# Two moves at the seam between attention and mixture of experts: one VectorE instruction later, one gather earlier

## The chip, the cores and the metric

The kernel runs on one core of one Trainium2 chip. The metric is the device time of one execution in microseconds (us). The engines are named as in the profile: PE (TensorE matmuls), PEld (its weight loads), DVE (VectorE), ACT (ScalarE), POOL (GpSimd) and SP (SyncE, which here only issues transfers).

## The reference

Causal attention with a cumulative bias over 8 batches of 8 heads (576 positions, 64 dimensions per head), whose output is the input of a mixture of 8 experts. Each of the 4608 rows goes to the one expert with the highest cosine similarity.

```
scores = q @ k^T / sqrt(D);  cum = cumsum(max(s, 0))
scores = where(causal, -1e9, scores + min(-(cum_i - cum_j), 0))
attn   = softmax(scores);    x = (attn @ v) as rows [4608, 512]
logits = xn @ en^T / tau;    expert_idx = argmax(logits);  gate_w = softmax(logits)[expert_idx]
for e in range(8):
    h = relu(x[expert_idx == e] @ w1[e]);  out[expert_idx == e] = gate_w * (h @ w2[e])
```

## The kernel before, in words

**Attention.** The 64 heads are a software pipeline: `step(n)` issues the scores of head n, the exponentials, the split of the probabilities into a 16-bit main part and a 16-bit remainder, and the product with V of head n-2. The remainder of the probabilities, `pl_`, is computed in pieces, by POOL (`psub`, L252) or by DVE (L508). The product, `pv`, accumulates in one PSUM bank, `om`; DVE's `norm1` to `norm3` (L539, L543, L551) read it out into the row buffer `xt`, and the next head's `pv` waits for that.

**Routing.** After the last head of a batch, `router` sums the logits out of `xt` (L79), picks the expert (L608 to L623), ranks the rows with matmuls (`rank0`, L630 to L636), and POOL scatters the rows to a list per expert in DRAM (`scat`, L670).

**Experts.** An expert's rows come back in five blocks of 128 (blocks 0 to 4). `xload(e, t)` (L739) is an indirect gather that POOL issues, into one of three places of 580 words in the tile `Qx`: place t % 3. `xprep(e, t)` then transposes the block on PE (L767, four matmuls), splits it on ACT and DVE (L775, L783) and takes its statistics (L751 on ACT; L748, L749, L79 on DVE); after that the place is free. `l1` multiplies with w1 (L915, L917), `l2m` with w2 (L986), and `l2o` scales a finished block on DVE (L993) and has POOL scatter it to the output (L994). Expert 0 begins while the attention ends: `first_pass(m)` is block m of its hidden layer for the first 256 rows, and the other rows follow in two more passes.

**Weights.** SP loads 128x512 pieces of w1 and w2, numbered q in the order of use, into a ring of raw buffers (`rw` is the tile of pieces 0 to 2). ACT converts a piece to 16 bits (`wcv`, L881) and DVE takes the remainder (`wlow`, L889), which also lets SP load a later piece into the freed buffer. `wlow(k)` takes the oldest k remainders that are pending.

**Order.** Each engine executes its instructions in the order in which the Python code issues them: the order is written out by hand and no scheduler changes it. Around the change that code is `step(n)` for n = 62 and 63 (the last two heads; `wlow(1)` at L1244), the lines behind the loop (L1400 to L1412), the closures `third`, `fourth` and `fifth`, which are called from the middle of expert 0's second-layer blocks, and the loop over m in expert 0's last first-layer pass (L1535 to L1537). POOL's queue holds remainders of probabilities, scatters, gathers and output scatters in one line.

Of the kernel before, what the change touches and what calls it, by code (L numbers as in the profile page):

```python
# [41 lines left out]
XR = 580  # L42
# [72 lines left out]
def main(ctx, tc, qkh, qkc, vtin, s_in, emb, tau, w1h, w2h, out, shared, nb):  # L115
# [36 lines left out]
    NH, LA = nb * H, 5  # L152
# [580 lines left out]
            X[("i", e, t)] = (xf[:, i], (IX["gi0"][:, t:t + 1], IX["va0"][:, t:t + 1]) if e + t0 == 0 and t1 < NTL else (IX["gi"][:, e, t:t + 1], IX["va"][:, e, t:t + 1]), L[:, i], ss[:, i], ex[:, :, t - t0])  # L733

    def xload(e, t):
        x = HT["Qx"][:, XR * (t % 3):XR * (t % 3) + XR]
        early = e == 0 and t < NF
        src = xs[0:SPL if t < 2 else SPM, :] if early else xs
        ins = nc.gpsimd.indirect_dma_start(out=x.bitcast(I32), out_offset=None, in_=src, in_offset=bass.IndirectOffsetOnAxis(ap=X[("i", e, t)][1][0].bitcast(U32), axis=0),  # L739
                                           bounds_check=src.shape[0] - 1, oob_is_err=False).ins  # L740
        X[("r", e, t)] = x
        if early:
            firsts.append(ins)
# [41 lines left out]
    def xprep(e, t, pt=None):  # L785
        xset(e, t)
        x = X[("r", e, t)][:, 0:XW]
        if e > 1:
            if "xr" not in HT:
                HT["xr"] = const.tile([128, 2, 2, 4, 128], F16, tag="KC1", name="xr")  # L790
            rows = x.rearrange("p (q c) -> p q c", q=4)[:, :, 8:136]
            h, l = (HT["xr"][:, t % 2, i] for i in range(2))
            nc.scalar.copy(h, rows)
            nc.vector.tensor_tensor(l, rows, h, op=ALU.subtract)
            for o, r in ((X[("H", e)], h), (X[("L", e)][1], l)):
                nc.sync.dma_start_transpose(o[:, :, 128 * t:128 * t + 128], r.rearrange("p q c -> p (q c)"))
            return xstat(e, t)
        xtr(e, t, pt)
        xcv(e, t)
        xstat(e, t)  # L800
# [85 lines left out]
    def wlow(k=99):  # L886
        for _ in range(min(k, len(lows))):
            q, l, a, s, h = lows.popleft()
            nc.vector.scalar_tensor_tensor(l, a, s, h, op0=ALU.mult, op1=ALU.subtract)  # L889
            wissue(min(q + 15, X.get("hold", 16 * NE)))  # L890
# [308 lines left out]
    def step(n):  # L1199
        m = n + LA - (n < 6)  # L1200
        live = n < NH
        b0, b1, c8 = n // H, n // H + 1, n % H
        prev = n - 1 < NH
        g, c = n // HG, n % HG
        if live and c == 0:
            hset(g + 1)
            if n > 4:
                load(g + 2)
                loadc(g + 2)
        if n == 10:  # L1210
            setup4()
            setup3()
        fslot()
        norm1(n - 3)
        if live:
            ta_(n, m)
        if prev:
            pl_(n - 1, 576, PS(n), "p")
        sr(m, 3)
        norm2(n - 3)  # L1220
        sa(m)
        if live:
            expa(n)
            prep(n, True)
        norm3(n - 3)
        if NH - 7 < n < NH:
            brk[0] = False
            slots(4)
        if live:
            tb_(n)  # L1230
        sr(m, 2)
        if live and n % 2 == 0:
            tbm(n)
        s3(m)
        if live:
            if n % 2:
                tbm(n)
            tbl(n)
        if n < NH - 6 or n >= NH:
            mslot()  # L1240
        if prev and PS(n) < 1600:
            pl_(n - 1, PS(n), 1600, "v")
        if n < NH - 1:
            wlow(1)  # L1244
        k = n - NH + 8
        if k == 3:
            wsq(8, True)
        if n < NH - 1:
            emm(n)
        sb(n, m)  # L1250
        sbr(m)
        if n < NH:
            tail(n)
        if n == 5:
            s1(10)
            sr(10, 3)
            s2(10)
        if n == 7:
            vscale(1)
        pv(n - 2, [0, 1, 2])  # L1260
        if n == 7:
            fslot()
        if rq:
            rq.popleft()()
        if n == 5:
            sr(10, 2)
            sr(10, 1)
            s3(10)
        pv(n - 2, [3, 4])
        if n == NH - 1:  # L1270
            emm(n)
        if n == 5:
            s4(10)
        if NH - 7 < n < NH:
            mslot()
        if n >= NH - 1:
            for f in (norm1, norm2, norm3):
                f(n - 2)
        if live:
            expb1(n)  # L1280
            if k == 7:
                wsq(13)
            vcp(n, False)
        if k == 3:
            wsum(0)
        aslot()
        if n == 4:
            load(3)
            loadc(3)
        if live:  # L1290
            prep(n, False)
            vcp(n, True)
        if n == NH - 1:
            xcv(0, 0)
            xtr(0, 1, pxs())
            xcv(0, 1)
        if k > 0:
            wsq((0, 2, 5, 8, 9, 10, 11, 14)[k])
            wcv((0, 0, 0, 0, 2, 1, 2, 1, 1, 1, 0)[k], True)
        brk[0] = False  # L1300
        if n < NH - 6:
            slots(4)
        if n in (4, 5, 6):
            vsq(1, ((0,), (1, 2), (3,))[n - 4])
        if H <= n < NH and 2 <= c8 < 6 and b1 < nb:
            vsq(b1, (c8 - 2,))
        if live and c8 == 6 and 1 < b1 < nb:
            vscale(b1)
        if n == 3:
            loadt(1, pair(1))  # L1310
        if H <= n < NH and c8 < 4:
            loadt(b1, c8)
        if n == NH - 9:
            wissue(3)
        for _ in range(SCN[c8] if n < NH - 22 else 2 if NH - 3 < n < NH else 1 + (c8 > 5) + 4 * (n > NH - 6)):
            scatter()
        later()
        if live and c == 0:
            addl(g + 1, True)
        if live and c == 1:  # L1320
            addl(g + 1, False)
        mrow1(m)
        if live:
            pl_(n, 0, 576, "p")
# [81 lines left out]
    wlow(1)  # L1406
    first_pass(0)
    wsq(16)
    wlow(1)
    pv(NH - 1, range(5))  # L1410
    wn = wparts()
    wn.pop(0)()  # L1412
# [77 lines left out]
    def fifth():  # L1490
        size(0)
        xprep(1, 2, pxm())
        wsq(22)
    l2(0, 1, {2: third, 4: partial(l2o, 0, 0, y), 6: fifth})
    l2(0, 2, {2: fourth, 7: l1t})
# [2 lines left out]
    for e in range(NE):  # L1498
        nx = e + 1 < NE
        w2, w1 = 16 * e + 8, 16 * e + 16  # L1500
        for m in range(8):
            l1(m, e, 0 if e else SPM, MAIN)
            if e > 1 and m == 1:
                l2u(e - 1)
            if e == 1 and m == 0:
                l2o(0, NTL - 1, X["y", 0])
            if e and m == 2:
                size(e)
            if e == 1:
                wsq(w2 + (6, 7, 8)[m] if m < 3 else w1 + (0, 0, 0, 1, 4)[m - 3])  # L1510
                if m == 3:
                    wn = wparts()
                    for i, f in enumerate(X[("g", 1, 0)][4]):
                        if i < len(wn):
                            wn[i]()
                        f()
                wcv((1, 2, 1, 2, 2, 2, 2, 0)[m])
            elif e > 1:
                if e == 2 and m == 0:
                    wsq(w2 + 8)  # L1520
                    wnorm()
                if e == 2 and m < 5:
                    wcv(2 if m else 0)
                if e > 2 and m < 4:
                    wcv(2)
                if nx and m > 3:
                    wsq(w1 + 2 * (m - 3))
            if nx and e > 0 and m == 1:
                xinfo(e + 1, 0, NTL)
            if nx and e > 0 and m == 2:  # L1530
                for t in range(3):
                    xload(e + 1, t)
            if e == 0 and m in (2, 4, 6):
                wsq(24 + m // 2)
            if e == 0 and m in (1, 5):  # L1535
                xprep(1, m // 4, pxm())
                xload(1, 3 + m // 4)  # L1537
            if e > 1 and m < 4:
                X[("g", e, 0)][m]()
            if e == 1 and m in (0, 4, 7):  # L1540
                X[("g", e, 0)][{0: 0, 4: 2, 7: 3}[m]]()
            if not nx and m == 5:
                nc.gpsimd.drain()
            if not nx and m == 4:
                xf = X[("i", e, NTL - 1)]
                nc.vector.tensor_copy(shared["last"][:, 0:1].bitcast(I32), xf[0])
                nc.vector.tensor_mul(shared["last"][:, 1:2], xf[3], IX["RS"][:, 2 * e + 1:2 * e + 2])
            if nx and e > 0 and m in (5, 7):
                xprep(e + 1, m // 2 - 2)
                xload(e + 1, m // 2 + 1)  # L1550
            if e == 2 and m == 5:
                count()
            if e == 3 and m == 4:
                shared["total"] = nc.values_load(shared["ci"][0:1, NE - 1:NE], min_val=0, max_val=NT // 128)
# [170 lines left out]
```

## Time and profile before

| | us |
|---|---|
| median of 3 runs | 760.83 |
| lowest, highest | 760.51, 762.04 |
| the profiled execution | 760.35 |
| its span, first to last instruction | 758.6 |
| PE busy | 738.8 (97% of the span) |
| ACT busy | 567.7 (75%) |
| DVE busy | 531.3 (70%) |
| POOL busy | 396.7 (52%) |

The profiled execution lasts 1.75 us longer than its span. Attention ends near 347 us on PE, and the experts follow. Where the profile shows an idle time in square brackets, it is the idle time of that engine just before the instruction, and behind the arrow stands what ended it.

### The profile page before, as it was taken

To read this page: it belongs to the slowest core of one execution; us is meant where nothing else is said; L and a number is where in the kernel's file an instruction comes from. 1 tells how busy PE (TensorE), PEld (TensorE's weight loads), DVE (VectorE), ACT (ScalarE), POOL (GpSimd) and SP (SyncE) were. 2 spreads that over 40 slices of the span, in tenths; PEclk is the share of its full clock that TensorE was granted. 3 is DMA by queue.
4 is the path that set the end of the run, shared out by engine and by line. 5 is a ranking of instruction groups with operands and counts; after the bars stand their busy time and mean duration, and the time that the engine had idled before them with its cause. 6 is when DMAs were issued, how large, how long until landed. Compare 5 with 4: busy or idle time off the path is not lost. (4 is left out here: it accounts for less than half of the span.)

```text
span 758.6 us, 20953 instructions
## 1 busy us (share of the span) xinstructions
PE 738.8 (97%) x7992; PEld 536.2 (71%) x7992; DVE 531.3 (70%) x1818; ACT 567.7 (75%) x1029; POOL 396.7 (52%) x377
## 2 busy tenths in 40 slices
PE   8999999999999999989989999999999999999996
PEld 4799999999999999978555454545454554554554
DVE  8778888888888888898767767565665566745621
ACT  9898989898999999977667878737658578475410
POOL 9997898989897988685323212222221122312011
PEclk9999999999999999999999999999999999999999
DMA  7789879797979797763625956845755657553001
GB/s 151 176 191 193 172 181 204 179 208 170 210 182 207 165 221 164 183 225 138 213 91 182 191 162 195 185 131 151 178 173 132 189 173 194 168 128 96 13 15 58
DMA packets 76002, 124.01 MB, mean 163 GB/s; under 512 B 38823, under 2 KB 39231, under 8 KB 75032
## 3 DMA queue, kind: packets, MB, share of 16 engines
q0 software_dynamic: 19632, 69.69, 39.1%
q1 hardware_dynamic: 56260, 52.84, 25.8%
q8 instruction: 71, 1.16, 0.7%
q14 instruction: 39, 0.32, 0.2%
HBM read 93.99 MB, written 21.49 MB: 152 GB/s over the span
## 5 line engine op out<-in xcount | busy, mean ns | idle before, releaser
L252 POOL TENSOR_TENSOR PL<-P 128x576 f16<-128x576 f32 (+2 forms) x128 | 204.5, 1719 | 13.6 <-ACT P L498 9.1
L915 PE MATMUL pe<-xH,wt 128*128 128x512 f16 (+1 forms) x576 | 153.0, 344 | 0.6 <-PEq L1020 0.5
L994 POOL DMA_INDIRECT out<-Kx,xj x39 | 43.0, 1103 | 201.6 <-DVE Kx L993 164.3
L915 PEld LDWEIGHTS <-wt 128*128 128x128 f16 x960 | 86.0, 98 | 81.6 <-issue 2.0
L526 PE MATMUL om<-vh,P 128*128 128x73 f16 x960 | 106.8, 198 | 2.7 <-DVE xt L551 2.0
L527 PE MATMUL om<-vl,P 128*128 128x72 f16 x960 | 106.2, 196 | 0.0
L528 PE MATMUL om<-vh,PL 128*128 128x73 f16 x960 | 106.0, 197 | 0.0
L739 POOL DMA_INDIRECT Qx<-xs,idx x40 | 47.5, 1188 | 101.8 <-ACT vjunk L844 44.9
L362 PE MATMUL s<-qkb 96*128 96x288 f32 (+4 forms) x272 | 96.2, 368 | 1.9 <-DVE M L370 0.8
L527 PEld LDWEIGHTS <-P 128*128 128x128 bf16 x960 | 94.6, 99 | 3.6 <-issue 3.2
L915 PE MATMUL pe<-xL,wt 128*128 128x512 f16 (+1 forms) x288 | 95.6, 344 | 0.0
L526 PEld LDWEIGHTS <-P 128*128 128x128 bf16 x960 | 93.8, 99 | 0.5 <-DVE xt L551 0.3
L528 PEld LDWEIGHTS <-PL 128*128 128x128 f16 x960 | 93.8, 98 | 0.0
L917 PE MATMUL pxs<-xH,wt 128*128 128x64 f16 x432 | 83.2, 193 | 0.0
L370 DVE CUSTOM_DVE_ANT_0 junk<-s,mS 128x448 bf16<-128x448 f32 (+3 forms) x144 | 73.9, 520 | 5.0 <-PE s L362 2.8
L986 PE MATMUL pxs<-wt,hq 128*128 128x512 f16 x297 | 72.7, 379 | 0.0
L501 ACT ACTIVATE P<-tb 128x1024 f32<-128x1024 f32 x64 | 65.1, 1017 | 3.3 <-PE tb L467 1.9
L986 PEld LDWEIGHTS <-hq 128*128 128x128 f16 x360 | 35.3, 98 | 42.0 <-ACT idx L88 0.3
L917 PEld LDWEIGHTS <-wt 128*128 128x128 f16 x648 | 63.5, 98 | 0.4
L464 PE MATMUL tb<-QC,KC 128*128 128x448 f32 (+3 forms) x256 | 63.3, 306 | 0.0
L460 PE MATMUL tb<-qkb 128*128 128x448 f32 (+3 forms) x256 | 61.2, 287 | 0.0
L889 DVE SCALAR_TENSOR_TENSOR wt<-ring,idx,wt 128x512 f16<-128x512 f32 x80 | 56.8, 745 | 4.8 <-ACT wt L881 4.8
(335 smaller groups left out, 1997.0 us busy)
## 6 DMA issues: line engine op xcount, KB each, us to landing
qkb<-qkh POOLq DMA_DIRECT2D x15, 1216.0 KB, 9.1
ring<-w2h SPq DMA_DIRECT2D x44, 256.0 KB
ring<-w1h SPq DMA_DIRECT2D x36, 256.0 KB
KC<-qkh POOLq DMA_DIRECT2D x14, 576.0 KB, 8.9
QC<-qkh POOLq DMA_DIRECT2D x14, 576.0 KB, 8.5
vT<-vtin SPq DMA_DIRECT2D x24, 320.0 KB
rw<-w1h SPq DMA_DIRECT2D x15, 256.0 KB
rw<-w2h SPq DMA_DIRECT2D x12, 256.0 KB
```

The source lines that it names most:

```text
L252: nc.gpsimd.tensor_tensor(out, a, b_, op=ALU.subtract)
L362: nc.tensor.matmul(out, G[g]["QB"][0:96, h, 128 * i:128 * i + 128], G[g]["KB"][0:96, h, lo:hi], start=True, stop=True)
L370: nc.vector.tensor_tensor_reduce(out=jk, in0=src, in1=ms, scale=1.0, scalar=NEG, op0=ALU.add, op1=ALU.max, accum_out=MP[n // 2][:, n % 2, ...
L460: nc.tensor.matmul(out, G[g]["KB"][:, h, ks:ks + 128], G[g]["QB"][:, h, 64 + qlo:64 + qhi], start=start, stop=False)
L464: nc.tensor.matmul(out, HD[n]["KC"][:, ks:ks + 128], HD[n]["QC"][:, qlo:qhi], start=False, stop=stop)
L501: nc.scalar.activation(HD[n]["P32"][:, 576:1600], HD[n]["tb"], AF.Exp, scale=0.125)
L526: nc.tensor.matmul(out, lh, vh[:, kb], start=(kb == 0), stop=False)
L527: nc.tensor.matmul(out[:, u:u + 72], lh, vl[:, kb], start=False, stop=False)
L528: nc.tensor.matmul(out, ll, vh[:, kb], start=False, stop=(kb == j))
L915: nc.tensor.matmul(h, w[:, 128 * c:128 * c + 128], x[:, c, lo:hi], start=(i == 0), stop=(i == 11))
L917: nc.tensor.matmul(X["a"][:, HALF * m:HALF * m + HALF], w[:, 128 * c:128 * c + 128], x[:, c, hi:hi + HALF], start=(i == 0), stop=(i == 11))
L986: nc.tensor.matmul(y, h, w, start=(m == 0 and k == 0), stop=(m == 7 and k == 2))
```

## The change

Three things are edited. In `step(n)`, the remainder of one weight piece is no longer taken at n = 62 (the last step but one). Behind the loop, the second `wlow` call takes two remainders where it took one, so that the count is made up behind `first_pass(0)`. For expert 1 the gather of block 3 uses place 2 and that of block 4 place 0 (before: places 0 and 1). Block 3 is gathered from `fifth`, behind the preparation of expert 1's block 2; block 4 is gathered at m = 1 of expert 0's loop, where block 3 was gathered before, and nothing is gathered at m = 5. Instructions are neither added nor taken away.

```diff
     def xload(e, t):
-        x = HT["Qx"][:, XR * (t % 3):XR * (t % 3) + XR]
+        i = t % 3 if e != 1 or t < 3 else (t - 1) % 3
+        x = HT["Qx"][:, XR * i:XR * i + XR]
...
-        if n < NH - 1:
+        if n < NH - 2:
             wlow(1)
...
     wlow(1)
     first_pass(0)
     wsq(16)
-    wlow(1)
+    wlow(2)
     pv(NH - 1, range(5))
...
     def fifth():
         size(0)
         xprep(1, 2, pxm())
+        xload(1, 3)
         wsq(22)
...
             if e == 0 and m in (1, 5):
                 xprep(1, m // 4, pxm())
-                xload(1, 3 + m // 4)
+                if m == 1:
+                    xload(1, 4)
```

On DVE, in the steps 62 and 63 of the kernel before, the remainder of piece 1 (the tile `rw_176`) stands between a part of head 61's probability remainder (L508) and the V remainder of head 62 (L311), and `norm1` to `norm3` of head 60 follow:

```order
L551 TENSOR_TENSOR xt<-om,z 128x5x72
L508 TENSOR_TENSOR PL_111<-P_87 128x576
L889 SCALAR_TENSOR_TENSOR wt<-rw_176,idx,wt 128x512
L311 SCALAR_TENSOR_TENSOR vl<-V,sc,vh_109 128x3x144
L539 TENSOR_SCALAR z<-om 128x5
L543 RECIPROCAL z<-z 128x5
L551 TENSOR_TENSOR xt<-om,z 128x5x72
```

Behind the loop, DVE has in the kernel before the read-out of head 62, piece 2's remainder, the first hidden block's low part (L922), piece 3's remainder, and the read-out of head 63:

```order
L543 RECIPROCAL z<-z 128x5
L551 TENSOR_TENSOR xt<-om,z 128x5x72
L889 SCALAR_TENSOR_TENSOR wt<-rw_177,idx,wt 128x512
L922 SCALAR_TENSOR_TENSOR hp<-h,hp 128x256
L889 SCALAR_TENSOR_TENSOR wt<-wt,idx 128x512
L539 TENSOR_SCALAR z<-om 128x5
```

The same place of the changed kernel (its lines behind the edit in `xload` are one higher, so L889 is L890 there):

```order
L543 RECIPROCAL z<-z 128x5
L551 TENSOR_TENSOR xt<-om,z 128x5x72
L890 SCALAR_TENSOR_TENSOR wt<-rw_176,idx,wt 128x512
L923 SCALAR_TENSOR_TENSOR hp<-h,hp 128x256
L890 SCALAR_TENSOR_TENSOR wt<-rw_177,idx,wt 128x512
L890 SCALAR_TENSOR_TENSOR wt<-wt,idx 128x512
L539 TENSOR_SCALAR z<-om 128x5
```

Piece 1's remainder has gone from the first place to the second, where it stands ahead of the first hidden block, and piece 2's remainder has moved behind that block; the instructions in between have kept their order.

On POOL, in the kernel before, the queue from the gathers ahead of expert 0's second layer to those of expert 2 (L739 gathers, L994 scatters output):

```order
L739 DMA Qx<-xs,idx 128x580 x3
L1461 MEMSET ring 1x1
L739 DMA Qx<-xs,idx 128x580
L994 DMA out<-Kx,xj 4608x512 x2
L739 DMA Qx<-xs,idx 128x580
L957 UNCONDITIONAL_BRANCH
L994 DMA out<-Kx,xj 4608x512
L739 DMA Qx<-xs,idx 128x580 x2
L967 UNCONDITIONAL_BRANCH
```

The same stretch of POOL's queue in the changed kernel (L740 and L995 are the gathers and the scatters):

```order
L740 DMA Qx<-xs,idx 128x580 x3
L1462 MEMSET ring 1x1
L740 DMA Qx<-xs,idx 128x580
L995 DMA out<-Kx,xj 4608x512
L740 DMA Qx<-xs,idx 128x580
L995 DMA out<-Kx,xj 4608x512
L740 DMA Qx<-xs,idx 128x580
L958 UNCONDITIONAL_BRANCH
L995 DMA out<-Kx,xj 4608x512
L740 DMA Qx<-xs,idx 128x580
L968 UNCONDITIONAL_BRANCH
```

One gather (expert 1's block 3) has moved ahead by one output scatter, one other gather (expert 1's block 1), the branch and a second output scatter; one gather (block 4) is left behind that scatter. On PE, ACT and SP the order is unchanged.

## Rows read from the trace of the kernel before

**Rows 1.** Part 1 of the page: engine, busy us (share), instructions.

```profile
PE 738.8 (97%) x7992; PEld 536.2 (71%) x7992; DVE 531.3 (70%) x1818; ACT 567.7 (75%) x1029; POOL 396.7 (52%) x377
```

**Rows 2.** What PE waited for, whole span: us in total, times, longest.

```profile
PE pxs L767 <- DMA Qx<-xs,idx: 3.0, 1, 3.0
PE om L526 <- DVE xt L551: 2.0, 1, 2.0
```

**Rows 3.** Timeline, PE, 335 to 353: start us, us, engine, line, what.

```profile
335.86 0.27 PE L467 MATMUL ta<-trim,identb 128*128 128x256 bf16 x1
...
337.74 0.60 PE L767 MATMUL pxs<-ident,Qx 128*128 128x128 f32 x4
340.31 0.19 PE L526 MATMUL om<-vh,P 128*128 128x73 f16 x1 [1.97 <-DVE xt L551]
...
345.85 0.20 PE L526 MATMUL om<-vh,P 128*128 128x73 f16 x1
...
352.32 0.18 PE L630 MATMUL om<-oh,tri 128*128 128x40 bf16 x1
```

**Rows 4.** Timeline, DVE, 323 to 352.

```profile
323.39 0.50 DVE L311 SCALAR_TENSOR_TENSOR vl<-V,sc,vh 128x288 f16<-128x288 f32 x1
...
334.95 3.87 DVE L889 SCALAR_TENSOR_TENSOR wt<-rw,idx,wt 128x512 f16<-128x512 f32 x1
...
339.32 0.15 DVE L539 TENSOR_SCALAR z<-om 128x5 f32<-128x5 f32 x1
...
339.73 0.53 DVE L551 TENSOR_TENSOR xt<-om,z 128x360 f32<-128x360 f32 x1
...
345.67 0.74 DVE L889 SCALAR_TENSOR_TENSOR wt<-rw,idx,wt 128x512 f16<-128x512 f32 x1
...
351.27 0.19 DVE L623 TENSOR_TENSOR oh<-wsel,idx 128x40 bf16<-128x40 f32 x1
```

**Rows 5.** Timeline, POOL, 321 to 344.

```profile
321.42 4.80 POOL L252 TENSOR_TENSOR PL<-P 128x576 f16<-128x576 f32 x4 [3.27 <-ACT P L498]
...
335.24 3.02 POOL L252 TENSOR_TENSOR PL<-P 128x576 f16<-128x576 f32 x2
...
340.97 3.02 POOL L252 TENSOR_TENSOR PL<-P 128x576 f16<-128x576 f32 x2
```

**Rows 6.** Timeline, ACT, near 334.

```profile
334.55 0.63 ACT L310 ACTIVATE vh<-V,sc 128x432 f16<-128x432 f32 x1 [0.43 <-PE V L300]
```

**Rows 7.** Timeline, PE, 385 to 398.

```profile
385.45 0.61 PE L767 MATMUL pxm<-ident,Qx 128*128 128x128 f32 x4
...
387.18 0.22 PE L915 MATMUL pe<-xH,wt 128*128 128x128 f16 x1
390.36 1.12 PE L767 MATMUL pxs<-ident,Qx 128*128 128x128 f32 x4 [2.96 <-DMA Qx<-xs,idx]
...
397.60 0.60 PE L767 MATMUL pxm<-ident,Qx 128*128 128x128 f32 x4
```

**Rows 8.** Windows: engines' busy us, then PE's granted clock, DMA share, GB/s.

```profile
338.00:340.30 2.30, 0.34 (x4) 0.17 (x2) 2.19 (x5) 2.27 (x5) 1.82 (x3) 1.00 0.17 28
390.00:392.00 2.00, 1.64 (x7) 1.18 (x8) 0.00 (x0) 0.49 (x2) 0.00 (x0) 0.54 0.51 149
392.00:394.00 2.00, 2.00 (x7) 0.77 (x6) 1.87 (x14) 1.28 (x6) 0.00 (x0) 0.61 0.00 0
```

**Rows 9.** Timeline, POOL, 374 to 388.

```profile
374.79 1.01 POOL L994 DMA_INDIRECT out<-Kx,xj  x1 [0.30 <-issue]
379.66 0.99 POOL L994 DMA_INDIRECT out<-Kx,xj  x1 [3.86 <-DVE xj L79]
380.95 1.04 POOL L739 DMA_INDIRECT Qx<-xs,idx  x1 [0.30 <-issue]
...
386.70 1.04 POOL L739 DMA_INDIRECT Qx<-xs,idx  x1 [0.30 <-ACT xH L775]
```

**Rows 10.** Timeline, DVE, the last reader of expert 1's block 2.

```profile
375.48 0.31 DVE L79 TENSOR_REDUCE xj<-Qx 128x8 f32<-128x64 f32 x1
```

## The prediction, made before the changed kernel ran

> **What bounds the kernel now.** Read part 1 of the page first: PE is busy for 97% of the span, no other engine for over 75% [rows 1]. So the time is PE's work plus the few places where PE stands still, and an edit off PE is worth only what it takes from such a place. Read next what PE waited for. Two waits lead the list, each a single event: 3.0 us for a gather into `Qx`, and 2.0 us for the read-out of `om` (L551) [rows 2]. Both lie where the change works. The timelines around them then show who made them.
>
> The shorter wait: PE is done with the transposes at 338.34 (337.74 + 0.60) and starts the product of head 61 at 340.31 [rows 3], when the read-out of head 60 has ended at 340.26 (339.73 + 0.53). DVE began that read-out at 339.32, because a weight remainder that takes 0.74 us elsewhere (the one at 345.67) took 3.87 from 334.95 [rows 4]. Meanwhile POOL ran two probability remainders, 335.24 to 338.26 [rows 5], and DVE's instruction ended 0.56 behind them: the stretch of 3.13 us is the time of POOL's pair.
>
> The longer wait: PE has nothing between 387.40 and 390.36, then transposes expert 1's block 3 [rows 7]. Its gather was issued at 386.70 [rows 9], so it landed at most 3.66 us later. After this wait PE's granted clock is low: 0.54 and 0.61 in two windows of 2 us [rows 8], a mixture of the levels 1.2 and 2.4 GHz. After the shorter wait it stayed at 1.00.
>
> **Edit 1, the remainder.** Removed from step 62: 3.87 us on DVE. L311 then starts when ACT's copy ends, 335.18 (334.55 + 0.63) [rows 6]. An L311 ran 0.50 us for 288 columns while POOL was in its four remainders (321.42 to 326.22) [rows 4, 5]; I take 0.75 for 432 columns, to 335.93. The read-out also needs head 60's product, behind which PE turns to other work at 335.86 [rows 3]; with 0.2 for its last matmul (PE's short rows are 0.18 to 0.22) that is 336.06. From L539's start to L551's end the read-out took 0.94 (339.32 to 340.26), so it ends near 337.0, with 1.3 us to spare before PE's 338.34. The wait goes: **1.97 us**.
>
> What is late next, with PE 1.97 earlier: head 63's product would start at 343.88 instead of 345.85 [rows 3], but POOL's last pair, which it needs, ends at 343.99 [rows 5], and POOL does not move. That is 0.1 us, with the signal perhaps 0.2.
>
> Added behind the loop: the same remainder, now ahead of `first_pass(0)`'s low part. DVE gets there near 343.7 (345.67 less 1.97), 0.3 before POOL's pair ends. By the nearest rows it costs DVE 0.74 at least and 3.87 at most; I take 0.74 + 0.3, the pair being almost over. On DVE's queue behind it stand the low part, two more remainders and the read-out of head 63, which leads to `oh`. PE's `rank0` waits for `oh`, and there are 0.86 us between them now (351.46 to 352.32). So 1.04 less 0.86 leaves 0.2 at most, and PE's own 0.1 to 0.2 just before covers it. For both together I take 0.2. No SP order changes; piece 1's buffer is refilled some 5 us later, for use tens of us on, at nothing. Edit 1: 1.97 - 0.2 = **1.77 us**.
>
> The Trainium skill (SBUF — State Buffer, "Who interferes with whom") says that a VectorE instruction with two SBUF inputs contends with a GpSimd instruction that reads SBUF, and that whichever issues first holds the pair of ports for its whole instruction. The 3.87 us agree that one blocks the other, but here DVE's instruction is shown starting 0.29 before POOL's and was still the one that waited. By the rule as by the row the new place costs 0.3 more, as long as POOL's pair is nearly through; where it is not, the rule makes the first rival below.
>
> **Edit 2, the gathers.** Block 3 takes the place of block 2, whose last reader on DVE ends at 375.79 (375.48 + 0.31) [rows 10]. POOL is idle from 375.80 to 379.66 [rows 9], and the gather's 1.04 + 0.30 fits into these 3.86 us. It lands by 376.1 + 1 + 3.66 = 380.8 even with a us lost, and PE asks for it at 387.4. Nothing else that PE's transposes need is shown late. So 2.96 us go, and with them the slow clock: (1 - 0.54) x 2 + (1 - 0.61) x 2 = 1.70, less what falls into the 0.36 us of window one that PE still idled: 1.6. Edit 2: 2.96 + 1.6 = **4.56 us**.
>
> What the moved instructions pass: the gather now stands ahead of the output scatter at 379.66, which starts then for a reason of its own, and of block 1's gather at 380.95. The latter lands by 384.61, and PE wants it at 385.45 [rows 7, 9]: 0.84 us of slack, unused by an insertion that POOL's idle time hides. Block 4's gather, formerly behind 386.70's, takes that issue slot and lands by 390.36; PE, 4.56 earlier, asks at 393.0 (397.60 - 4.56). Slack 2.7 us, cost nothing. The gather's traffic falls between others'; from the rows it could cost block 1's landing anything from nothing to one gather's 1.34 us, of which 0.84 is covered. I take nothing, the row of the idle 3.86 us being nearest.
>
> **Sum.** 1.77 + 4.56 = 6.33 us. The profiled execution of 760.35 us would become 754.0. The median of the runs is 760.83, 0.48 above it, so the predicted median is **754.5 us**. The list of waits names no other of this size for the expert stage, so I expect what is won to stay.
>
> **Rivals.**
>
> 1. *The port again.* If DVE reaches the moved remainder with POOL's last pair still ahead (POOL later by some 3 us, or DVE earlier), it is stretched by 3.13 once more, `oh` comes about 3 us late for `rank0`, and edit 1 turns from 1.77 gained into 1 lost: 760.83 - 4.56 + 1.0 = 757.3. If merely another wait refills the place at 338.3, it is 760.83 - 4.56 = 756.3. For it: the row of 3.87. Against: the head's product that DVE needs first ends no sooner than POOL's pair allows, and POOL's queue in that stretch is unchanged. Chance 0.13.
> 2. *Block 1 instead of block 3.* If the inserted gather is not hidden, block 1's gather is up to 1.34 late, and with its slack of 0.84 PE stands 0.5 us at 385.45: 755.0. At 3 us of delay the wait is 2.2 and the time 756.7. Chance 0.08.
> 3. *Slower.* POOL's queue is in order. If the new gather is held until H by a count of another engine that is reached only late, everything behind it waits: block 1's gather starts at H + 2.63 (1.04 + 0.30 + 0.99 + 0.30 [rows 9]), lands 3.66 later, and PE stands for H - 379.2 at its 385.45. With the low clock behind it (1.6) this eats the whole 6.33 at H = 383.9 and makes the kernel slower by 0.2% from H = 385.4, 9.6 us behind the last reader. At H = 387 the time is 760.83 - 6.33 + 7.8 + 1.6 = 763.9. Against: all readers of place 2 are done by 376. Chance 0.03.
> 4. *Edit 2 does nothing*, because the wait at 390.36 was ended by something that the profile put down to the gather: 760.83 - 1.77 = 759.1. Against: issue and landing fit. Chance 0.03.
>
> **How the numbers follow.** The forecast has 0.73, its own range 753.8 to 755.2. The low end of the range is all idle and clock time gone with nothing given back (1.97 + 2.96 + 1.70 = 6.63) and a half us that I don't see: 753.5 or a little less. The high end takes in rivals 1 and 2: 757.4. A difference of 0.2% (1.5 us) is what a measurement of this kernel can tell from none. Faster by more than that are the forecast, rivals 1 and 2, and half of rival 4: 0.955, of which I move 0.025 to no change for what I don't see; with the other half of rival 4 that is 0.04. Slower is rival 3.
>
> **What would show it.** In the changed kernel's profile PE's list of waits lacks both leading rows; no weight remainder on DVE lasts over 1.2 us near the seam; expert 1's block 3 is gathered about 10 us before its transposes; and the granted clock stays at 1.00 through expert 0. I am wrong if PE stands over 0.5 us at `rank0`, at the transposes of block 1, or at head 61's product.

## The result, and the profile after

The changed kernel took 754.34 us (median of 5 runs, 753.1 to 754.6) against 762.04 (5 runs, 760.51 to 762.95) of the kernel before on the same chip: a ratio of 0.9899 [0.9883, 0.9916] (in brackets, here and below, the 95% interval), or 6.4 to 8.9 us less. The prediction was 754.5 us. The profiled execution lasted 753.1 us with a span of 751.4; before it was 760.35 and 758.6. Lines below L736 are one higher than before (L890 is the former L889, L740 the former L739, L768 the former L767).

Part 1 of the page of the changed kernel answers to [rows 1]: PE's busy time fell by 1.1 us only; the other 6.1 us by which the span shrank had been idle time.

```profile
PE 737.7 (98%) x7992; PEld 535.9 (71%) x7992; DVE 528.0 (70%) x1818; ACT 567.3 (76%) x1029; POOL 395.6 (53%) x377
```

The head of PE's list of waits (us in total, times, longest), to be held against [rows 2]: both waits of before are gone, and what leads now lies at other places of the program.

```profile
PE pm L448 <- DVE es L590: 1.5, 1, 1.5
PE om L207 <- DVE tiny L186: 1.3, 1, 1.3
PE s L362 <- DVE M L370: 0.9, 3, 0.4
```

PE at the seam, in the timeline of the changed kernel (start, us, engine, line, what), answering to [rows 3]:

```profile
337.49 0.60 PE L768 MATMUL pxs<-ident,Qx 128*128 128x128 f32 x4
...
337.92 0.20 PE L526 MATMUL om<-vh,P 128*128 128x73 f16 x1
...
349.93 0.18 PE L630 MATMUL om<-oh,tri 128*128 128x40 bf16 x1
```

Head 61's product follows the start of the transposes by 0.43 us; before it was 2.57 (337.74 to 340.31). `rank0` starts 2.39 earlier than before, of which 0.25 was there already at 337.49.

DVE in the same stretch, answering to [rows 4]: the read-out of head 60 ends at 336.77, and the moved remainder (343.27) takes 0.77 us.

```profile
334.96 0.67 DVE L311 SCALAR_TENSOR_TENSOR vl<-V,sc,vh 128x432 f16<-128x432 f32 x1 [0.18 <-ACT vh L310]
...
336.24 0.53 DVE L551 TENSOR_TENSOR xt<-om,z 128x360 f32<-128x360 f32 x1
...
343.27 0.77 DVE L890 SCALAR_TENSOR_TENSOR wt<-rw,idx,wt 128x512 f16<-128x512 f32 x1
...
349.38 0.19 DVE L623 TENSOR_TENSOR oh<-wsel,idx 128x40 bf16<-128x40 f32 x1
```

POOL, answering to [rows 5, 9]: the second pair ends at 343.49, 0.22 behind the start of the moved remainder. The gather at 374.26 is block 3's, 10.6 us ahead of its transposes; the one at 378.84 is block 1's.

```profile
335.00 3.02 POOL L252 TENSOR_TENSOR PL<-P 128x576 f16<-128x576 f32 x2
...
340.47 3.02 POOL L252 TENSOR_TENSOR PL<-P 128x576 f16<-128x576 f32 x2
...
374.26 1.03 POOL L740 DMA_INDIRECT Qx<-xs,idx  x1 [0.84 <-ACT vjunk L845]
377.52 1.01 POOL L995 DMA_INDIRECT out<-Kx,xj  x1 [2.23 <-issue]
378.84 1.02 POOL L740 DMA_INDIRECT Qx<-xs,idx  x1 [0.30 <-PE pe L963]
```

PE's transposes of expert 1's blocks 1, 3 and 4, answering to [rows 7]: none has an idle time in front.

```profile
383.11 0.61 PE L768 MATMUL pxm<-ident,Qx 128*128 128x128 f32 x4
...
384.90 0.60 PE L768 MATMUL pxs<-ident,Qx 128*128 128x128 f32 x4
...
390.54 0.60 PE L768 MATMUL pxm<-ident,Qx 128*128 128x128 f32 x4
```

The windows behind block 3's transposes (length, busy us of PE, PEld, DVE, ACT, POOL with counts, then the granted clock, the DMA share and GB/s), answering to [rows 8]: full clock.

```profile
386.00:388.00 2.00, 2.00 (x11) 0.93 (x10) 1.82 (x12) 1.39 (x5) 0.00 (x0) 1.00 0.35 97
388.00:390.00 2.00, 2.00 (x11) 0.94 (x10) 1.82 (x10) 1.89 (x4) 0.00 (x0) 1.00 0.00 0
```

How far PE is ahead of its trace before, place by place: 0.25 us at 337.49 (ahead of the change, from one execution to another), 2.39 at head 61's product, 2.34 at block 1's transposes, 5.46 at block 3's, 7.06 at block 4's. So edit 1 gave 2.14, the gather's wait 3.12 and the clock behind it 1.60.

### The profile page after: what moved, and what is told of

It reads as the page before. It is cut to its first block, busy times and chain, and to the rows that moved or that the text cites. A ratio compares the mean times of both kernels' runs of the same rounds, so it can differ in the third digit from the quotient of the medians.

```text
span 751.4 us, 20953 instructions
## 1 busy us (share of the span) xinstructions
PE 737.7 (98%) x7992; PEld 535.9 (71%) x7992; DVE 528.0 (70%) x1818; ACT 567.3 (76%) x1029; POOL 395.6 (53%) x377
## 5 line engine op out<-in xcount | busy, mean ns | idle before, releaser
L995 POOL DMA_INDIRECT out<-Kx,xj x39 | 42.8, 1098 | 197.4 <-DVE Kx L994 158.9
L526 PE MATMUL om<-vh,P 128*128 128x73 f16 x960 | 106.8, 199 | 0.7 <-DVE base L641 0.3
L740 POOL DMA_INDIRECT Qx<-xs,idx x40 | 46.9, 1171 | 102.9 <-ACT vjunk L845 45.3
L526 PEld LDWEIGHTS <-P 128*128 128x128 bf16 x960 | 93.8, 99 | 0.5 <-DVE xt L551 0.3
L890 DVE SCALAR_TENSOR_TENSOR wt<-ring,idx,wt 128x512 f16<-128x512 f32 x80 | 56.8, 746 | 4.6 <-ACT wt L882 4.6
```

Of the source, the lines that this page charges most:

```text
L526: nc.tensor.matmul(out, lh, vh[:, kb], start=(kb == 0), stop=False)
```

## The experiments

They ran on three chips. rem_only, gather_only, busy_wait and rem_behind ran on one where the kernel before took 761.49 us (17 runs), much as in the first comparison; no_pair, gather_twice, place_only and q0_behind on a second, where it took 766.17 (28 runs); the four whose names end in _again on a third, where it took 765.65 (23 runs). Ratios are to the kernel before on the same chip; the only trace of the kernel before is the one that the prediction read. The two theories: the stretched remainder held head 60's read-out, and the late gather held block 3 and with it cost the clock. The rivals are named with each run.

**Each edit alone: rem_only and gather_only.** rem_only is the kernel before with edit 1:

```diff
-        if n < NH - 1:
+        if n < NH - 2:
             wlow(1)
...
-    wlow(1)
+    wlow(2)
     pv(NH - 1, range(5))
```

> Edit 1 alone (the weight remainder leaves step 62), gathers as before. My theory (two separate waits of PE): the 2.0 us wait for L551 is gone, the 3.0 us wait for the gather and the slow clock behind it stay; 2.0 to 2.2 us less than before, near 758.7 where before is 760.8. Rival (both edits work only together, because PE that comes earlier just waits longer for the gather): the gather wait grows to about 5 us and the time is within 0.5 us of before.

Measured: 758.49 us (6 runs), ratio 0.9961 [0.9947, 0.9975], so 1.9 to 4.0 us less. The wait at L551 is gone; the gather's stays and the clock falls behind it. The head of PE's list of waits, a row of PE's timeline, and its windows:

```profile
PE pxs L767 <- DMA Qx<-xs,idx: 3.3, 2, 2.8
```

```profile
389.14 1.05 PE L767 MATMUL pxs<-ident,Qx 128*128 128x128 f32 x4 [2.85 <-DMA Qx<-xs,idx]
```

```profile
388.00:390.00 2.00, 0.86 (x5) 0.80 (x6) 0.00 (x0) 0.00 (x0) 0.52 (x1) 0.81 0.40 107
390.00:392.00 2.00, 2.00 (x7) 0.77 (x6) 1.16 (x7) 1.59 (x5) 0.00 (x0) 0.50 0.13 49
392.00:394.00 2.00, 2.00 (x9) 0.87 (x8) 1.86 (x14) 1.46 (x3) 0.00 (x0) 0.83 0.00 0
```

gather_only is edit 2 without edit 1, that is the changed kernel with

```diff
-        if n < NH - 2:
+        if n < NH - 1:
             wlow(1)
...
-    wlow(2)
+    wlow(1)
     pv(NH - 1, range(5))
```

> Edit 2 alone (expert 1's blocks 3 and 4 gathered into the places in the order in which they come free), the remainder stays in step 62. My theory: the 2.0 us wait and a DVE remainder of about 3.9 us stay, the 3.0 us wait is gone and PE's granted clock stays at 1.00 behind it; 4.6 us less than before, near 756.2 where before is 760.8. Rival (another gather takes the place): a wait of 0.5 us or more at the transposes of block 1 or 4, and under 4 us less.

Measured: 757.74 us (6 runs), ratio 0.9958 [0.9946, 0.9970], so 2.3 to 4.1 us less: by the runs under the 4.6 expected, though the profiled execution's span (753.6) is 5.0 below that of the trace before. In its trace the remainder is stretched again and PE waits for the read-out; neither block 3 nor block 1 or 4, the ones that the rival named, is waited for:

```profile
PE om L526 <- DVE xt L551: 2.0, 1, 2.0
```

```profile
334.73 3.87 DVE L890 SCALAR_TENSOR_TENSOR wt<-rw,idx,wt 128x512 f16<-128x512 f32 x1
```

The two edits therefore act at separate places, each on its own wait. By the ratios they sum to 6.2 us (4.2 to 8.1 by the two intervals), against 6.4 to 8.9 for both together in the first comparison.

**What stretched the remainder: no_pair and rem_behind.** no_pair is the kernel before without POOL's two remainders of head 62; that part of the probabilities is left out of the computation:

```diff
-        if prev:
+        if prev and n != NH - 1:
...
-        if live:
+        if live and n != NH - 2:
```

> The kernel before without POOL's two probability remainders of head 62 (left out of the computation), so that the weight remainder in step 62 has nothing beside it on POOL. My theory (the 3.87 us are the time in which POOL's pair holds what DVE needs): the remainder in step 62 takes 0.75 us, PE's wait for L551 is gone, and the gather wait stays; about 2 us less than before. Rival (the remainder waited for its operands or was slow by itself): still near 3.9 us and PE's wait of 2.0 us.

Measured: 764.71 us against 766.17, ratio 0.9980 [0.9968, 0.9993]. The remainder falls from 3.87 to 0.74 us, at the same place and on the same data. So POOL's pair is what stretched it. DVE's rows in its timeline:

```profile
335.15 0.74 DVE L889 SCALAR_TENSOR_TENSOR wt<-rw,idx,wt 128x512 f16<-128x512 f32 x1
...
338.77 0.16 DVE L539 TENSOR_SCALAR z<-om 128x5 f32<-128x5 f32 x1 [2.31 <-PE ta L464]
```

The time fell by 0.5 to 2.5 us. The read-out of head 60 still began late, at 338.77, and now with 2.31 us of idle DVE in front that PE ended; PE itself came late to the transposes (338.86), and its wait at L526 was 0.3 us, where the trace before has 2.0. So this run shows what stretched the remainder, and not what the stretch cost PE. The gather's wait stays (3.2 us).

rem_behind is the changed kernel with piece 1's remainder back in step 63, but behind head 60's read-out instead of ahead of it:

```diff
+        if n == NH - 1:
+            wlow(1)
...
-    wlow(2)
+    wlow(1)
     pv(NH - 1, range(5))
```

> The changed kernel, but piece 1's remainder is taken in step 63 behind the read-out of head 60, so still while POOL runs its pair of probability remainders, and one remainder instead of two behind the first hidden block. My theory (the position ahead of the read-out cost PE, not the stretch as such): the remainder is stretched until POOL's pair ends, so some 1.5 to 2.5 us instead of 0.75, nobody waits for it, and the time is that of the changed kernel within 0.5 us. Rival (a stretched remainder costs PE wherever it stands in this stretch): PE's wait for L551 is there again and the time is 1.5 to 2 us above the changed kernel's.

Measured: 754.19 us (4 runs), ratio 0.9912 [0.9895, 0.9929]: the gain of the changed kernel. DVE's and POOL's rows:

```profile
336.19 0.53 DVE L551 TENSOR_TENSOR xt<-om,z 128x360 f32<-128x360 f32 x1
336.64 1.88 DVE L890 SCALAR_TENSOR_TENSOR wt<-rw,idx,wt 128x512 f16<-128x512 f32 x1
```

```profile
334.94 3.02 POOL L252 TENSOR_TENSOR PL<-P 128x576 f16<-128x576 f32 x2
```

The remainder is stretched here too, to 338.52, which is 0.56 us behind the end of POOL's pair (337.96). PE doesn't notice, because nothing that it needs soon stands behind it. What cost PE was the place ahead of the read-out, not the stretch in itself.

The 0.56 comes back in each case. In the kernel before the remainder ends at 338.82, 0.56 behind 338.26 [rows 4, 5]; in gather_only at 338.60, 0.56 behind the pair that started there at 335.02; in the changed kernel the moved one ends at 344.04, 0.55 behind 343.49. POOL's pair took 3.02 us in all of them. So in these traces the remainder, whether shown inside the pair or up to 0.29 ahead of it, ends when POOL's pair has ended and 0.55 to 0.56 us have passed.

The Trainium skill (SBUF — State Buffer, "Who interferes with whom") says that issue order decides who blocks, and, of VectorE's two-port modes, that whichever issues first has the shared ports for its whole instruction. rem_behind agrees: POOL was first and DVE waited. In the kernel before DVE is shown starting first, by 0.29 us, and still waited, for both of POOL's instructions. There the rule doesn't describe what the rows show, unless a start in the rows is not yet the issue that it means; no run here tells that.

**Whether idle time lowers the clock: busy_wait.** The kernel before with 12 matmuls, whose result nobody reads, put ahead of block 3's transposes:

```diff
+                    if t == 3:
+                        z = pe()
+                        for _ in range(12):
+                            nc.tensor.matmul(z, wt(1, 0)[0][:, 0:128], X[("H", 0)][:, 0, 0:MAIN], start=True, stop=True)
```

> The kernel before, with 12 matmuls of 512 columns into a spare bank added ahead of the transposes of expert 1's block 3 (about 2.6 us of PE work whose result nobody reads), so that PE is busy during most of its wait for the gather. My theory: the landing sets the start of the transposes, which stay where they were, but PE's granted clock stays at 1.00 behind them; 1.6 us less than before although work was added, near 759.2 where before is 760.8. Rival (the low clock does not come from the idle time): clock near 0.5 for some 3 us as before, and the same time as before.

Measured: 759.21 us (12 runs) against 761.49, ratio 0.9973 [0.9960, 0.9986], so 1.1 to 3.0 us less for 2.75 us of added work. PE's timeline, and the window that was at 0.54 before [rows 8]:

```profile
387.35 2.75 PE L1565 MATMUL pe<-xH,wt 128*128 128x512 f16 x12
390.87 0.66 PE L767 MATMUL pxs<-ident,Qx 128*128 128x128 f32 x4 [0.77 <-DMA Qx<-xs,idx]
```

```profile
390.00:392.00 2.00, 1.23 (x9) 0.80 (x9) 0.00 (x0) 0.43 (x1) 0.00 (x0) 1.00 0.57 162
```

Block 3 is no earlier (390.87 against 390.36), and the time falls. From block 3's transposes to block 4's PE took 5.70 us (to 396.57) instead of 7.24 [rows 7]. The runs say the same as the one trace: the mean granted clock over the span was 0.997 or more in 9 of the 12, and in only one of the 17 of the kernel before on that chip. So the clock's share in the wait's price is real, and filling the wait takes most of it away.

**Whether a second gather would have made block 1 late: gather_twice.** The changed kernel with block 3 gathered twice, so that POOL's queue has one gather more ahead of block 1's:

```diff
         xload(1, 3)
+        xload(1, 3)
         wsq(22)
```

> The changed kernel with block 3's gather of expert 1 issued twice in a row into the same place; the second waits on POOL for the landing of the first, so POOL's idle time no longer hides it. My theory: the second starts near 378, block 1's gather near 380.6 instead of 378.8, lands near 384.4, and PE waits 1 to 1.7 us at block 1's transposes (383.1) with its clock still at 1.00; 1 to 1.7 us above the changed kernel. Rival (POOL has more room there than its row shows): no wait there over 0.3 us and the changed kernel's time.

Measured: 763.95 us against 766.17 there, ratio 0.9971 [0.9961, 0.9980]. The changed kernel did not run on that chip, so the expected difference to it is not measured. POOL's rows (the second gather of block 3, the scatter and block 1's gather), and PE's:

```profile
382.87 1.01 POOL L740 DMA_INDIRECT Qx<-xs,idx  x1 [3.14 <-DMA Qx<-xs,idx]
384.19 1.01 POOL L995 DMA_INDIRECT out<-Kx,xj  x1 [0.31 <-issue]
385.51 1.03 POOL L740 DMA_INDIRECT Qx<-xs,idx  x1 [0.30 <-issue]
```

```profile
389.30 0.63 PE L768 MATMUL pxm<-ident,Qx 128*128 128x128 f32 x4 [1.21 <-DMA Qx<-xs,idx]
```

The mechanism of rival 2 exists: a gather that POOL's idle time does not hide costs PE 1.21 us at block 1. In the changed kernel it is hidden.

**Whether the early issue or the place does it: place_only, changed_again and place_only_again.** The changed kernel with block 3's gather back at m = 1, into the new place:

```diff
         xprep(1, 2, pxm())
-        xload(1, 3)
         wsq(22)
...
                 if m == 1:
+                    xload(1, 3)
                     xload(1, 4)
```

> The changed kernel, but block 3's gather of expert 1 is issued where it was before (at m = 1, with block 4's behind it): the new places, the old position in POOL's queue. My theory (the place only permits the early issue; in the old position the gather still stands behind the third output scatter): the gather starts 1.3 us behind that scatter, near 384 in this kernel's time, lands some 3.6 us later, PE waits 2.5 to 3 us at block 3's transposes and its clock falls behind; 755.5 to 759 against 754.3 for the changed kernel. Rival (the gather was late because its old place came free late): no wait of over 0.5 us, the changed kernel's time.

Measured: 761.89 us against 766.17, ratio 0.9963 [0.9944, 0.9983], and no wait for the gather: the expectation missed. Since the changed kernel had not run on that chip, both ran together on a third one:

> The changed kernel once more, as the yardstick for the three kernels beside it. Theory: 6.3 to 7.7 us below the kernel before on the same chip (ratio 0.990 to 0.992), with neither of the two waits. Rival, that the gain of the first comparison was partly the chip's: less than 5 us (ratio over 0.9935). On a chip where PE shows idle stretches of 1.5 to 2 us ended by its own sequencer, as in the four kernels run together before, the difference would be 4 to 5 us, since there the gather's wait is shorter.

> The changed kernel with block 3's gather issued where it was before (m = 1 of expert 0's loop), into the new place. Theory, that the early issue is what removes the wait and the place only allows it: issued near 384 us, landing 3.7 us later, PE stands 2.5 to 3.0 us ahead of block 3's transposes, and with the low clock behind it the kernel is 3 to 4.6 us slower than the changed one of the same call. Rival, that the place frees the gather by itself: same time as the changed kernel within 1 us and no wait over 0.5 us.

Measured against 765.65: changed_again 760.86 (6 runs), ratio 0.9946 [0.9929, 0.9964]; place_only_again 761.77 (12 runs), 0.9965 [0.9944, 0.9985]. The expectation of 3 to 4.6 us between them missed again: the medians are 0.9 apart and the intervals overlap. In the trace of place_only_again POOL's queue and PE show why:

```profile
384.76 0.99 POOL L995 DMA_INDIRECT out<-Kx,xj  x1 [1.56 <-DVE hq L949]
386.06 1.04 POOL L740 DMA_INDIRECT Qx<-xs,idx  x1 [0.30 <-issue]
```

```profile
389.11 0.22 PE L916 MATMUL pe<-xL,wt 128*128 128x128 f16 x1
...
389.89 0.61 PE L768 MATMUL pxs<-ident,Qx 128*128 128x128 f32 x4
```

The gather starts 0.64 us earlier than in the kernel before [rows 9], and PE, which is late on this chip, asks for the block at 389.89, 2.5 us later than the 387.4 of before. The difference 389.89 - 386.06 = 3.83 us is about what a gather took where PE waited for it (3.66 at most before, 3.79 in gather_twice). The median is not the whole of it, though. Three of the twelve runs of place_only_again took 766.1 to 767.3 us, as long as the kernel before, at a mean granted clock of 0.996 to 0.997; the other nine took 761.0 to 762.1 at 0.998 to 1.0. Four of the ten of place_only lie at 763.8 to 766.9. None of the six runs of changed_again lies above 763.4. A gather that comes too late in some executions would do this, but no trace of a long run exists, so it is not shown. How much the early issue is worth where PE is not late, these runs do not tell either: that was not run on such a chip.

changed_again itself missed the 6.3 to 7.7 us expected, and its rival holds: the gain depends on the chip, 2.8 to 5.4 us here, 6.4 to 8.9 in the first comparison. Rows of PE's list of waits, of its timeline and of DVE's:

```profile
PE pxs L942 <- issue: 1.9, 6, 0.5
PE pe L916 <- issue: 1.6, 2, 1.0
PE om L526 <- DVE xt L551: 1.6, 1, 1.6
```

```profile
340.25 0.73 PE L300 MATMUL V<-en,vT 128*128 128x144 f32 x4
340.81 0.60 PE L768 MATMUL pxs<-ident,Qx 128*128 128x128 f32 x4
342.98 0.21 PE L526 MATMUL om<-vh,P 128*128 128x73 f16 x1 [1.56 <-DVE xt L551]
```

```profile
341.97 0.17 DVE L539 TENSOR_SCALAR z<-om 128x5 f32<-128x5 f32 x1 [4.37 <-PE pxs L768]
```

"issue" is idle time that nothing in the profile ends; all its entries in the list come to 3.9 us here and 0.3 in the changed kernel's first trace. The third row is a wait for a read-out again, one head later, and it is not the port: no weight remainder stands there. PE turned from the product of head 61 to other work at 340.25, and DVE saw it done only at 341.97, 1.7 us later (0.2 in the first trace: 339.43 and 339.63). DVE was idle for 4.37 us before, and ACT, which waited for V, was released late too, at 342.02. PE's own signal was late, and what held it the profile does not show. The wait is in all six traces of kernels with edit 1 from the second and third chip (1.5 to 2.0 us), and in none of the three from the first comparison and the first chip. So in the traces from those two chips much of what edit 1 frees is taken again at once.

**The same idle time on two chips: no_pair_again.** no_pair once more, because its trace had shown 3.2 us of waiting and no low clock.

> The kernel before without POOL's two probability remainders of head 62 (left out of the computation). In the earlier run, on another chip, DVE's weight remainder took 0.74 us and 3.2 us of waiting for the gather were followed by a granted clock of 1.00. Theory A, that an idle time of about 3 us on PE is followed by the low clock wherever it is: clock under 0.8 in two windows behind the wait, and the kernel 2.0 us faster than before. Theory B, that it depends on how the idle time lies and the low clock can stay away after 3 us: clock 1.00 there, and 3 to 3.6 us faster. The remainder takes 0.7 to 0.8 us in both.

Measured: 764.44 us (10 runs), ratio 0.9986 [0.9976, 0.9997], so 0.2 to 1.8 us less. The remainder takes 0.74 us again. PE's wait and its windows in no_pair:

```profile
391.97 0.66 PE L767 MATMUL pxs<-ident,Qx 128*128 128x128 f32 x4 [3.22 <-DMA Qx<-xs,idx]
```

```profile
390.00:392.00 2.00, 0.03 (x1) 0.03 (x1) 0.29 (x2) 0.45 (x3) 0.98 (x1) 1.00 0.50 146
392.00:394.00 2.00, 2.00 (x12) 1.16 (x13) 0.72 (x3) 1.34 (x4) 0.00 (x0) 1.00 0.32 118
```

and in no_pair_again:

```profile
391.28 0.66 PE L767 MATMUL pxs<-ident,Qx 128*128 128x128 f32 x4 [1.96 <-DMA Qx<-xs,idx]
```

```profile
390.00:392.00 2.00, 0.72 (x6) 0.61 (x7) 0.29 (x1) 0.19 (x3) 1.02 (x1) 1.00 0.19 76
392.00:394.00 2.00, 2.00 (x7) 0.78 (x6) 1.41 (x9) 1.57 (x5) 0.00 (x0) 0.59 0.57 149
394.00:396.00 2.00, 2.00 (x7) 0.69 (x5) 1.86 (x11) 1.71 (x3) 0.00 (x0) 0.56 0.00 0
```

The shorter wait was followed by the low clock and the longer one was not. Theory A falls as far as it goes by length: that an idle time of about 3 us is followed by the low clock wherever it is. Theory B stands, without what decides; the time came out as neither had it (2.0, and 3 to 3.6 us less). The ten runs of no_pair differ among themselves, too: the mean granted clock was 0.996 or 0.997 in six and 0.998 to 1.0 in four, so one trace of a kernel doesn't tell what its other executions do.

**Piece 0 as well: q0_behind and q0_behind_again.** The changed kernel with piece 0's remainder behind L311 in step 61:

```diff
-        if n < NH - 2:
+        if n < NH - 3:
             wlow(1)
...
+            if n == NH - 3:
+                wlow(1)
```

> The changed kernel with piece 0's remainder too taken later: in step 61 behind the V remainder of head 61 instead of ahead of it (it is stretched to 1.4 us by POOL there, and PE waits 0.4 us for that V remainder). My theory: PE's wait of 0.4 us before head 62's V product goes, and the time falls by 0.2 to 0.4 us, less than runs can tell. Rival (the read-out of head 60 or the V remainder becomes later through it): no change or 0.5 us more.

> The changed kernel with piece 0's remainder in step 61 behind the V remainder instead of ahead of it. Theory, that the 0.4 us for which PE waits at V on the V remainder is made by that remainder: this wait goes and the kernel is 0.2 to 0.4 us faster than the changed one, too little to tell. Rival, that the remainder behind L311 delays head 59's read-out: 0.3 to 1 us slower.

Measured: ratio 0.9959 [0.9943, 0.9974] (762.73 against 766.17), and beside the changed kernel 762.02 against its 760.86, ratio 0.9955 [0.9938, 0.9971] to the kernel before. No gain: PE's 0.5 us at V leaves the list, but the wait at L526 grows from 1.6 to 2.0. In q0_behind_again PE came to the transposes 0.43 us earlier than in changed_again (340.38 against 340.81), and DVE was released at 341.97 in both. The time is the same or a little worse. The changed kernel stays the best of those run, with rem_behind its equal.

## Why the prediction was right

**What bounds the kernel.** Right: the change took idle time of PE and little else, and no other engine's share moved by more than one point.

**Edit 1** was forecast at 1.97 - 0.2 = 1.77 us and gave 2.14. Both parts were a little off. The idle time of 1.97 in brackets begins at the end of the transposes, which the profile models, and back to back they overlap the product by 0.17 (0.60 less 0.43), which comes back too. The 0.2 set off did not fall due: POOL, which was taken not to move, ended its pair at 343.49 instead of 343.99, the moved remainder took 0.77 instead of 1.04, and `oh` ended at 349.57, 0.36 ahead of `rank0`. Of the 0.86 us of slack there, 0.50 was used. The working of the read-out held: 337.0 forecast, 336.77 measured. rem_only shows the edit by itself at 1.9 to 4.0 us.

**Edit 2** was forecast at 2.96 + 1.6 and gave 3.12 + 1.60, in the changed kernel's trace (the 0.16 is the same overlap). gather_only measured 2.3 to 4.1 for it in its runs, on another chip, so the size of 4.56 is not confirmed there; the mechanism is (no wait, clock 1.00). The clock's term was the boldest, and busy_wait showed it as a thing apart from the wait. By the prediction's own windows it is 1.70 less 0.17, so 1.53 and not 1.6; that 1.60 was measured is partly luck. That the low clock follows any wait of this length, no_pair refuted.

**What the moved instructions pass** cost nothing, as forecast: block 1's transposes came 2.34 us earlier and without a wait, block 4's without a wait.

**The sum** of 6.33 stands against 7.25 in the profiled executions: 0.25 from one execution to the other, 0.05 lost again ahead of block 1, 2.14, 3.12 and 1.60 as above, and 0.2 behind. The interval of the runs is 6.4 to 8.9, and the 6.33 lies just below it. That the predicted 754.5 and the measured 754.34 us are within 0.2 of each other is therefore partly luck: 6.33 was taken off 760.83, and the kernel before measured 762.04 beside the changed one. The low end of the prediction's range, 760.83 - 6.63 - 0.5, is 753.7 and not 753.5. "I expect what is won to stay" held here; it did not hold in full on the third chip (2.8 to 5.4 us), where PE had stops of its own. The prediction did not speak of another chip.

**The rivals.** The port again (1): the moved remainder did overlap POOL's pair, by 0.22 us, which by the 0.55 behind the pair's end leaves it at nearly its usual length; on the second and third chip another wait, one head later, did take much of it back, as in the second form of this rival, but PE's late signal made it. Block 1 (2): not here, and gather_twice shows the mechanism at 1.21 us, inside the forecast's 0.5 to 2.2. Slower (3): the gather started 0.84 us behind the work ahead of it and was not held. Edit 2 without effect (4): refuted by gather_only. The signs that were named appear: both waits gone, block 3 some 10 us early, clock 1.00, and no remainder over 1.2 us from 333 us on. Piece 0's remainder in step 61, which the edits leave where it was, still took 1.42 us at 331.36, as it did before at 331.61.

## What to carry to other kernels

When an instruction lasts several times its usual length, look at what the neighbouring engine ran in that time, and move the instruction behind whatever the bottleneck waits for; that it was still stretched there cost nothing here. Price a wait of PE together with the granted clock of the windows behind it, and take the clock's part as likely rather than certain. For a gather into rotating buffers, assign the buffer that comes free first and check that the queue it moves up in is idle long enough, since a gather that isn't hidden makes the next one late. What the early issue gives beyond the free buffer, these runs leave open.

## What the runs showed of the hardware that was not expected

- Three chips gave the kernel before 761.5, 766.2 and 765.7 us. In the traces from the slower two, PE's idle time ended by nothing in the profile comes to 3.4 to 4.5 us; in those from the first comparison and the first of the three chips, to 0.2 to 0.7.
- On those two chips PE's signal reached DVE late at one place in every trace with edit 1, by 1.7 us in changed_again (341.97), with DVE idle; in both traces of no_pair the read-out of head 60 began late (338.77 and 339.05), with 2.3 us of idle DVE in front. The cause is open.
- PE's granted clock fell after waits of 2.96 us (before), 2.85 (rem_only) and 1.96 (no_pair_again), and stayed at 1.00 after 1.97 (before, at L526) and 3.2 (no_pair). The length of the wait alone doesn't decide.
- DVE's remainder ended 0.55 to 0.57 us behind POOL's pair wherever it overlapped one, whether it was shown starting 0.29 ahead of it, 1.70 into it or 0.22 before its end. Such an overlap has a price that can be read off: the pair's end, plus 0.56, less the start.
